# Halved attention scores spread into a dense layer, and two reorderings of v pieces, in a one-core attention and dense kernel

## Chip, cores, metric

One core of one Trainium2 chip. The metric is the device time of one execution in microseconds (us), lower is better. Times of a kernel are medians over several executions. Ratios are the mean time of one kernel's fast runs over that of the other's fast runs of the same rounds, so they are not quite the ratios of the medians quoted.

Names in the profiles: PE is the matrix engine (PEld its weight loads), ACT and DVE are the two engines that in these kernels read PSUM, the memory that PE's results go to here, and apply exp, relu, sums and copies ("eviction" is such a copy out of PSUM), POOL is a fourth engine. The number in brackets at the end of a line is the idle time of the engine before it, and what ended it.

## The reference

Block-sorted attention, then a dense layer with a squared relu. Cut to what matters:

```python
# q, k, v: 4 batches x 8 heads x 768 x 64; sort_net: 4 x 8 x 8 x 8 ; block = 96 rows
P = sinkhorn(sort_net)                       # five rounds of row and column normalising
k_sorted = einsum('bhij,bhjcd->bhicd', P, k_b); v_sorted = the same with v_b
scores = scale * q_b @ k_sorted.T            # within each block of 96
attn = exp(scores - max) / sum
x = attn @ v_sorted                          # -> 3072 tokens x 512
out = (s * relu(x @ w_in)**2 + b) @ w_out    # 512 -> 2048 -> 512
```

## The kernel before

A batch of 768 tokens is two half batches (`t`) of four blocks. `s_piece` makes scores and exp for one pair of heads (`hp`) of a half batch, `p_piece` the weighted values ("pv") and their normalisation into x, `t_piece` the transposes of x, `ffn1` the first dense matmuls ("hps"), relu and square ("gt"), `ffn2` the second ("ops"). Attention of later half batches runs in `slot()`, between the matmuls of dense layers. All PSUM tiles come from two pools: `psa`, three buffers of 2 x 512 floats a row, and `psb`, two buffers of 512 floats a row.

```python
psa = tile_pool(name="psa", bufs=3, space=PSUM);  psb = tile_pool(name="psb", bufs=2, space=PSUM)

def s_piece(t, hp):                               # 8 matmuls, one exp of 96 x 768
    sc = psa.tile([BLK, 2, 512], FP, tag="a", name="sc")
    ...                                           # matmul per block n and head e of the pair
    at = atp.tile([BLK, 2, TG], BF, tag="at", name="at")
    nc.scalar.activation(out=at, in_=sc[:, :, 0:TG], func=AF.Exp, scale=scale)

def p_piece(t, hp, n0=0, nn=HB):                  # blocks n0 .. n0+nn
    if nn < HB: p1 = psb.tile(...)                # two blocks: the small pool
    else:       p2 = psa.tile(...)                # four blocks: the large pool
    ...                                           # matmuls at x vs
    nc.vector.reciprocal(out=rec, ...)
    nc.vector.tensor_tensor(out=x[...], in0=pv, in1=rec, op=ALU.mult)

def ffn1(t, slot=nothing, n0=0, nn=HB):
    for f0 in range(0, NF, 2):                    # 8 steps
        hps = psa.tile([128, 2, 512], FP, tag="a", name="hps")
        ...                                       # 8 matmuls
        nc.scalar.activation(out=rt, in_=hps, func=AF.Relu)
        nc.vector.tensor_tensor(out=gt, in0=rt, in1=rt, op=ALU.mult)
        slot()

# start: ... k and v pieces of batch 0, s_piece(0, 0..3) among the last v pieces, then the ladder:
for hp in range(NHP):
    p_piece(0, hp, 0, 2)
    if hp == 3: t_part(0, 0, "s", 0, 2)
    warm_up(2, psa)                               # two matmuls of 128 x 256 on zeros
t_part(0, 2, "v", 0, 2); warm_up(2, psa)
ffn1(0, Queue([P(0,0,2,2), P(0,1,2,2), P(0,2,2,2), P(0,3,2,2),
               q_half(1), t_piece(0,"v",2,2), SC(1,0), SC(1,1)], 8), 0, 2)   # blocks 0, 1
ffn1(0, Queue([...], 8), 2, 2)                                               # blocks 2, 3
...
# k pieces of batch 1 in ffn2(0): evicted by "vsv"[c0 // 32], v = DVE, s = ACT
```

The softmax here doesn't subtract the row's maximum and nothing guards it: scores larger than these inputs give would overflow.

## Time and profile before

| | before |
|---|---|
| median of 5 runs | 233.47 us (233.34 to 233.67) |
| span of the profiled run | 231.6 us |
| first pv matmul / first hps matmul | 23.71 / 27.32 us |
| fifth hps group / q transposes of the second half | 30.84 / 31.60 us |
| hps of the next dense layer | 47.08 us |
| ops matmuls behind the wait on ot | 70.32 us |

The positions are starts on PE. As PE is busy for 97% of the span, the difference of two such starts against another kernel tells what was won or lost between them. The lines of the profile that carry the argument are in the prediction.

### The profile page before, as it was taken

To read this page: it belongs to the slowest core of one execution; us is meant where nothing else is said; L and a number is where in the kernel's file an instruction comes from. 1 tells how busy PE (TensorE), PEld (TensorE's weight loads), DVE (VectorE), ACT (ScalarE), POOL (GpSimd) and SP (SyncE) were. 2 spreads that over 40 slices of the span, in tenths; PEclk is the share of its full clock that TensorE was granted. 3 is DMA by queue.
4 is the path that set the end of the run, shared out by engine and by line. 5 is a ranking of instruction groups with operands and counts; after the bars stand their busy time and mean duration, and the time that the engine had idled before them with its cause. 6 is when DMAs were issued, how large, how long until landed. Compare 5 with 4: busy or idle time off the path is not lost.

```text
span 231.6 us, 4837 instructions
## 1 busy us (share of the span) xinstructions
PE 224.3 (97%) x2036; PEld 136.8 (59%) x2036; DVE 116.8 (50%) x245; ACT 114.6 (49%) x164; POOL 48.3 (21%) x62
## 2 busy tenths in 40 slices
PE   8879999999999999999999999999999999999994
PEld 6779887765544555566555555665555556554442
DVE  5778566638992645244446653343452634432221
ACT  6168479685158486856630645656222236660000
POOL 7820000399992000007920000000000000000000
PEclk9975699999999999999999999999999999999999
DMA  5999999998799992764999995610115240001212
GB/s 93 142 200 211 226 193 205 231 220 183 106 110 180 273 312 63 161 82 65 130 148 133 183 197 115 93 47 0 46 47 113 93 110 4 3 0 45 80 59 91
DMA packets 46695, 28.90 MB, mean 125 GB/s; under 512 B 35921, under 2 KB 41041, under 8 KB 46161
## 3 DMA queue, kind: packets, MB, share of 16 engines
q0 software_dynamic: 18800, 15.21, 47.8%
q1 hardware_dynamic: 27728, 13.32, 26.6%
q8 instruction: 16, 0.26, 0.5%
q10 hardware_dynamic: 144, 0.07, 0.1%
q14 instruction: 7, 0.05, 0.1%
HBM read 29.63 MB, written 8.65 MB: 165 GB/s over the span
## 4 chain that ended last, share of the span: by engine, by line
PE 82%; DVE 7%; DMA 5%; ACT 3%; issue 1%; POOL 0%; POOLq 0%
PE hps L473 35%; PE ops L516 31%; DMA qr<-in_q_dram 5%; PE pv L402 4%; PE sc L375 3%; DVE gt L478 2%; ACT ks L240 2%; DVE ks L238 2%; PE tv L320 2%; PE ops L501 2%; PE tk L294 1%; PE tv L350 1%; PE wp L182 1%; PE tq L254 1%; PE tv L336 1%
## 5 line engine op out<-in xcount | busy, mean ns | idle before, releaser
L473 PE MATMUL hps<-xt,wi 128*128 128x384 bf16 (+1 forms) x576 | 87.1, 309 | 0.3 <-ACT rt L477 0.3
L516 PE MATMUL ops<-wo,gt 128*128 128x512 bf16 x368 | 86.9, 380 | 0.4 <-DVE ot L490 0.4
L473 PEld LDWEIGHTS <-wi 128*128 128x128 bf16 x576 | 54.1, 98 | 30.6 <-issue 1.3
L477 ACT ACTIVATE rt<-hps 128x768 bf16<-128x768 f32 (+1 forms) x72 | 53.1, 741 | 37.4 <-PE hps L473 37.0
L478 DVE TENSOR_TENSOR gt<-rt 128x768 bf16<-128x768 bf16 (+1 forms) x72 | 41.2, 574 | 50.2 <-ACT rt L477 50.0
L516 PEld LDWEIGHTS <-gt 128*128 128x128 bf16 x368 | 33.6, 98 | 37.2 <-issue 1.0
L378 ACT ACTIVATE at<-sc 96x768 bf16<-96x768 f32 x32 | 24.4, 804 | 27.7 <-PE sc L375 27.7
L490 DVE SCALAR_TENSOR_TENSOR ot<-ops,s_bc,bias 128x512 f32<-128x512 f32 x23 | 17.1, 749 | 41.2 <-PE ops L516 41.2
L240 ACT CAST ks<-tk 64x512 bf16<-64x512 f32 (+1 forms) x32 | 18.6, 582 | 10.5 <-PE tk L294 10.2
L407 DVE TENSOR_TENSOR x<-pv,rec 96x512 bf16<-96x512 f32 (+1 forms) x36 | 22.6, 627 | 1.3
L639 POOL TENSOR_TENSOR csum<-csum,wo 128x512 f32<-128x512 f32 x14 | 17.6, 1254 | 1.0
L402 PEld LDWEIGHTS <-at 96*128 96x128 bf16 (+1 forms) x256 | 12.0, 104 | 3.8
L182 PE MATMUL wp<-zt 128*128 128x256 bf16 x86 | 12.9, 311 | 1.1 <-DVE warm L113 1.1
L238 DVE CAST ks<-tk 64x512 bf16<-64x512 f32 (+1 forms) x20 | 13.0, 651 | 1.1 <-PE tk L294 0.8
L402 PE MATMUL pv<-vs,at 96*128 96x66 bf16 (+1 forms) x256 | 13.0, 199 | 0.1
L240 ACT CAST vn<-tv 128x512 bf16<-128x512 f32 (+1 forms) x12 | 9.4, 799 | 7.2 <-PE tv L350 5.0
L375 PEld LDWEIGHTS <-ks 64*96 64x96 bf16 x256 | 8.6, 128 | 5.8 <-issue 5.1
L406 DVE RECIPROCAL rec<-pv 96x8 f32<-96x8 f32 (+1 forms) x36 | 6.9, 192 | 9.5 <-PE pv L402 9.4
L84 POOL DMA_DIRECT2D qr<-in_q_dram x12 | 10.6, 912 | 4.8 <-DMA kb<-in_k_dram 3.1
L375 PE MATMUL sc<-qt,ks 64*96 64x96 bf16 x256 | 10.9, 219 | 0.1
L182 PEld LDWEIGHTS <-zt 128*128 128x128 bf16 x86 | 9.0, 110 | 2.6 <-DVE warm L113 1.1
L294 PEld LDWEIGHTS <-kb 64*128 64x128 bf16 x192 | 6.7, 99 | 3.9 <-issue 3.4
(73 smaller groups left out, 98.4 us busy)
## 6 DMA issues: line engine op xcount, KB each, us to landing
out_dram<-ot SPq DMA_DIRECT2D x23, 256.0 KB, 2.4
kb<-in_k_dram POOLq DMA_DIRECT2D x4, 768.0 KB, 12.2
vb<-in_v_dram POOLq DMA_DIRECT2D x4, 768.0 KB, 19.0
wi<-in_moe_w_in_dram POOLq DMA_DIRECT2D x2, 1024.0 KB, 19.7
wo<-in_moe_w_out_dram POOLq DMA_DIRECT2D x2, 1024.0 KB, 32.6
qr<-in_q_dram POOLq DMA_DIRECT2D x12, 128.0 KB, 13.5
dv<-vn SPq DMA_DIRECT2D x6, 256.0 KB, 7.5
vs<-dv POOLq DMA_DIRECT2D x4, 384.0 KB, 12.7
```

What stands on the lines that cost most here:

```text
L182: nc.tensor.matmul(out=wp, lhsT=zt[:, 0:128], rhs=zt, start=True, stop=True)
L238: nc.vector.tensor_copy(out=out, in_=in_)
L240: nc.scalar.copy(out=out, in_=in_)
L375: nc.tensor.matmul(out=sc[:, e, n * BLK:(n + 1) * BLK], lhsT=ks[pr, g0 + n, :], rhs=QT[b][pr, hp, q0:q0 + BLK], start=True, stop=True)
L378: nc.scalar.activation(out=at, in_=sc[:, :, 0:TG], func=AF.Exp, scale=scale)
L402: nc.tensor.matmul(out=pv[e][0:m, (n - n0) * VW:(n - n0 + 1) * VW], lhsT=atf[:, c0:c0 + m], rhs=VS[b][:, gi, :], start=True, stop=True)
L407: nc.vector.tensor_tensor(out=x[:, n0:n0 + nn, hp * 128:(hp + 1) * 128].rearrange("p n (e d) -> p e n d", e=2), in0=pvv[:, :, :, 0:D], in1 ...
L473: nc.tensor.matmul(out=hps[:, f, 0:nt], lhsT=wi_at(hp, f0 + f), rhs=xt_at(t, hp, n0, nn), start=(hp == 0), stop=(hp == NHP - 1))
L477: nc.scalar.activation(out=rt[:, :, 0:nt], in_=hps[:, :, 0:nt], func=AF.Relu)
L478: nc.vector.tensor_tensor(out=gt[:, f0:f0 + 2, c0:c0 + nt], in0=rt[:, :, 0:nt], in1=rt[:, :, 0:nt], op=ALU.mult)
L516: nc.tensor.matmul(out=ops, lhsT=gt[:, f, m * 128:(m + 1) * 128], rhs=wo_at(f), start=(f == 0), stop=(f == NF - 1))
L639: nc.gpsimd.tensor_tensor(out=csum, in0=csum, in1=wo_at(f), op=ALU.add)
```

## The change

The first scores are made in halves (two blocks each), so that only the halves which the ladder needs come before it. The other halves move into the first half of the dense layer, two pairs of heads in each of the first two steps; the second pv pieces, one per step before, then come two per step. Two reorderings sit next to waits: pv of pair 2 ahead of a v piece of batch 1, and a v piece of the later batches ahead of scores. The diff, cut to its core:

```diff
+    def s_half(t, hp, n0, nn=2):
+        sc = psa.tile([BLK, 2, 512], FP, tag="a", name="sc")
+        ...                                  # 4 matmuls
+        at = atp.tile([BLK, 2, nn * BLK], BF, tag="at", name="ath")
+        nc.scalar.activation(out=at, in_=sc[:, :, 0:nn * BLK], func=AF.Exp, scale=scale)
+        AT[t, hp, n0] = at
 # p_piece reads AT[t, hp, n0] where there is one
-    s_piece(0, 0)            # and pairs 1, 2, 3, among the last v pieces
+    s_half(0, 0, 0)          # the same
-    ffn1(0, Queue([P(0, 0, 2, 2), P(0, 1, 2, 2), P(0, 2, 2, 2), P(0, 3, 2, 2),
+    def SH(hp): return lambda: (s_half(0, hp, 2), s_half(0, hp + 1, 2))
+    ffn1(0, Queue([SH(0), SH(2), seq(P(0, 0, 2, 2), P(0, 1, 2, 2)),
+                   seq(P(0, 2, 2, 2), P(0, 3, 2, 2)),
                    lambda: q_half(1, "s"), lambda: t_piece(0, "v", 2, 2), SC(1, 0), SC(1, 1)], 8), 0, 2)
-    ... seq(SC(1, 3), P(1, 1)), V1(1), P(1, 2), P(1, 3), ...
+    ... seq(SC(1, 3), P(1, 1)), P(1, 2), V1(1), P(1, 3), ...
-    ... V2[0], S2(2, 0), V2[1], S2(2, 2), V2[2], V2[3], ...
+    ... V2[0], V2[1], S2(2, 0), V2[2], S2(2, 2), V2[3], ...
```

More of the change, by code (lines that the diff above doesn't have):

```diff
@@ L379, in s_piece @@
         AT[t, hp] = at
+    def s_half(t, hp, n0, nn=2):
+        b, half = divmod(t, 2)
+        g0 = (b % 2) * 32 + hp * NB + half * HB
+        sc = psa.tile([BLK, 2, 512], FP, tag="a", name="sc")
+        for n in range(n0, n0 + nn):
+            for e in range(2):
+                pr = slice(e * 64, (e + 1) * 64)
+                q0 = (half * HB + n) * BLK
+                nc.tensor.matmul(out=sc[:, e, (n - n0) * BLK:(n - n0 + 1) * BLK],
+                                 lhsT=ks[pr, g0 + n, :], rhs=QT[b][pr, hp, q0:q0 + BLK],
+                                 start=True, stop=True)
+        at = atp.tile([BLK, 2, nn * BLK], BF, tag="at", name="ath")
+        nc.scalar.activation(out=at, in_=sc[:, :, 0:nn * BLK], func=AF.Exp, scale=scale)
+        AT[t, hp, n0] = at
     def p_piece(t, hp, n0=0, nn=HB):
         b, half = divmod(t, 2)
-        at = AT[t, hp]
+        halved = (t, hp, n0) in AT
+        at = AT[t, hp, n0] if halved else AT[t, hp]
         if t not in X:
@@ L398, in p_piece @@
             for n in range(n0, n0 + nn):
-                c0 = (e * HB + n) * BLK
-                m = 128 if c0 + 128 <= 2 * TG else BLK
+                c0 = (e * nn + n - n0) * BLK if halved else (e * HB + n) * BLK
+                m = 128 if c0 + 128 <= at.shape[1] * at.shape[2] else BLK
                 gi = e * 32 + hp * NB + half * HB + n
@@ L594 @@
     v_piece0(32, 16, "v")
-    s_piece(0, 0)
+    s_half(0, 0, 0)
     v_piece0(48, 8, "v")
-    s_piece(0, 1)
+    s_half(0, 1, 0)
     v_piece0(56, 8, "v")
-    s_piece(0, 2)
-    s_piece(0, 3)
+    s_half(0, 2, 0)
+    s_half(0, 3, 0)
     for hp in range(NHP):
@@ L619, in V1, with SH @@
         return lambda: v_piece1(i * 8, eng)
-    ffn1(0, Queue([P(0, 0, 2, 2), P(0, 1, 2, 2), P(0, 2, 2, 2), P(0, 3, 2, 2),
+    def SH(hp):
+        return lambda: (s_half(0, hp, 2), s_half(0, hp + 1, 2))
+    ffn1(0, Queue([SH(0), SH(2), seq(P(0, 0, 2, 2), P(0, 1, 2, 2)),
+                   seq(P(0, 2, 2, 2), P(0, 3, 2, 2)),
                    lambda: q_half(1, "s"), lambda: t_piece(0, "v", 2, 2), SC(1, 0), SC(1, 1)], 8), 0, 2)
-    ffn1(0, Queue([seq(SC(1, 2), P(1, 0)), V1(0), seq(SC(1, 3), P(1, 1)), V1(1), P(1, 2), P(1, 3),
+    ffn1(0, Queue([seq(SC(1, 2), P(1, 0)), V1(0), seq(SC(1, 3), P(1, 1)), P(1, 2), V1(1), P(1, 3),
                    seq(V1(2), V1(3)), lambda: t_piece(1, "v")], 8), 2, 2)
@@ L652 @@
                + [lambda c0=c0: k_piece(1, c0, 16, 1, "vsv"[c0 // 32])() for c0 in range(0, BLK, 32)]
-               + [seq(lambda: load_q(2), lambda: load_k(*brows(2)), bias_piece), V2[0], S2(2, 0), V2[1], S2(2, 2), V2[2], V2[3],
+               + [seq(lambda: load_q(2), lambda: load_k(*brows(2)), bias_piece), V2[0], V2[1], S2(2, 0), V2[2], S2(2, 2), V2[3],
                   P2(2, 0), V2[4], P2(2, 2), V2[5], S2(3, 0),
```

## The prediction

> **What bounds the kernel now.** I read the page first (who is busy), then the waits of PE, the granted clock in narrow windows, and the timeline from 12 to 100 us, the only part that the change touches.
>
> ```profile
> PE 224.3 (97%) x2036; PEld 136.8 (59%) x2036; DVE 116.8 (50%) x245; ACT 114.6 (49%) x164; POOL 48.3 (21%) x62
> ```
>
> PE is the bound over the whole span, so a change is worth what it removes from PE's queue or from PE's waits, and costs what it adds there. The waits of PE are few; these two lie where the change acts:
>
> ```profile
> PE ops L516 <- DVE ot L490: 0.4, 1, 0.4
> PE hps L473 <- ACT rt L477: 0.3, 1, 0.3
> ```
>
> The timeline puts the 0.3 us wait before the matmuls at 42.99 us and the 0.4 us wait before those at 70.32 us. So the reorderings that the description calls "around waits" can win 0.9 us at the very most (counting by starts, 42.52 to 42.99 and 69.91 to 70.32). The windows show where PE runs at half clock:
>
> ```profile
> 14.00:16.00 2.00, 1.51 (x33) 1.35 (x28) 1.93 (x3) 1.99 (x4) 0.00 (x0) 0.53 0.95 157
> ...
> 26.00:28.00 2.00, 2.00 (x19) 1.70 (x17) 1.01 (x4) 0.48 (x1) 0.00 (x0) 0.56 1.21 246
> 28.00:30.00 2.00, 2.00 (x33) 1.86 (x31) 1.04 (x4) 0.98 (x2) 0.00 (x0) 1.00 1.01 203
> ```
>
> The first of the last three numbers is the granted clock: half from 14.2 us to about 27.9 us, full afterwards. The stage before the dense layer lies in the slow stretch, and what ends it is not the scores but v:
>
> ```profile
> 21.36 0.81 ACT L378 ACTIVATE at<-sc 96x768 bf16<-96x768 f32 x1 [0.65 <-PE sc L375]
> ...
> 22.97 0.69 DVE L238 CAST vs<-tv 96x512 bf16<-96x512 f32 x1 [0.20 <-PE tv L320]
> ...
> 23.71 0.38 PE L402 MATMUL pv<-vs,at 96*128 96x66 bf16 x4
> ```
>
> The first exp is done at 22.17 us, the last v eviction at 23.66, and the weighted values start at 23.71. From there to 27.32 the stage is a fixed ladder of pv, warm-up and transposes on PE, 0.65 us a step.
>
> Then the dense layer's first half, in which the second scores will have to go:
>
> ```profile
> 27.32 1.05 PE L473 MATMUL hps<-xt,wi 128*128 128x192 bf16 x8
> 28.20 0.30 PE L402 MATMUL pv<-vs,at 96*128 96x66 bf16 x4
> 28.34 0.83 PE L473 MATMUL hps<-xt,wi 128*128 128x192 bf16 x8
> 29.00 0.30 PE L402 MATMUL pv<-vs,at 96*128 96x66 bf16 x4
> ...
> 30.84 0.83 PE L473 MATMUL hps<-xt,wi 128*128 128x192 bf16 x8
> 31.60 0.94 PE L254 MATMUL tq<-ident,qr 64*64 64x64 bf16 x48
> ```
>
> By starts, eight hps matmuls occupy PE 0.66 us (28.34 to 29.00), four pv ones 0.14. A step is 0.80 to 0.88 us, and nothing waits more than 0.1. The pieces that feed ACT and DVE there, by form between 20 and 48 us:
>
> ```profile
> L477 ACT ACTIVATE rt<-hps 128x384 bf16<-128x384 f32 x16 | 7.8, 497 | 4.9 <-PE hps L473 4.6
> L378 ACT ACTIVATE at<-sc 96x768 bf16<-96x768 f32 x8 | 6.4, 808 | 1.0 <-PE sc L375 1.0
> ...
> L407 DVE TENSOR_TENSOR x<-pv,rec 96x256 bf16<-96x256 f32 x8 | 3.4, 420 | 0.3
> ```
>
> [...] The trace agrees (497 and 808), so I take 0.49 us for a halved exp, some 0.45 in a row. [...] the trace shows it where a ready normalisation waits behind the relu's square (pv of 41.31 us, its reciprocal at 42.31 after the square of 42.04). That order is what the step below rests on.
>
> **Part 1: the first scores in halves.** Four of eight matmuls and half of each exp leave the stage before the dense layer: 16 matmuls, some 0.8 us of PE at half clock (eight take 0.40 us there), and 4 x (0.81 - 0.49) = 1.3 us of ACT. On the path lies only this: the last v matmuls come eight sc matmuls, 0.4 us, earlier, but DVE is evicting the piece before until 22.78, so its 0.20 us of idle is all that is won. The dense layer then begins at 27.13 instead of 27.32, still at half clock: the 0.19 us is worth 0.09 us of work at full clock. Its first eight matmuls end at 28.11 instead of 28.20.
>
> **Part 2: the second halves in the dense layer.** Added to PE: 16 matmuls at full clock, 0.31 us for eight: 0.62 us. Added to ACT: four exps, two behind each of the first two relus. The scores and hps share three buffers of the large PSUM pool (pv pieces of two blocks use the small one, of two). Before, hps had all three to itself; now each step wants hps, sc, sc, so every next hps must wait for the relu of the one before. Step by step, with 0.2 us from the last matmul's issue to ACT:
> - hps0 ends 28.11; sc, sc to 28.42; relu0 28.31 to 28.80; exps to 29.25 and 29.69.
> - hps1 waits for relu0: 28.84 instead of 28.42 (wait 0.42), to 29.50. relu1 29.70 to 30.19. sc, sc 29.58 to 29.90, the second waiting for the second exp. Exps to 30.64 and 31.08.
> - hps2 waits for relu1: 30.23 (0.33), to 30.89. relu2, behind two exps, 31.09 to 31.58. Its square 31.62 on DVE.
> - The two pv pieces now together: PE 30.97 to 31.25. Their normalisations stand behind the square on DVE: first x done 32.51, second 33.06 (reciprocal and product some 0.55 us apart).
> - hps3 31.25 to 31.91. The next two pv pieces need the small pool's two buffers back: 32.55 (wait 0.64) and 33.10 (0.41), to 33.24.
> - hps4 at 33.32; it was 30.84.
>
> So +2.48 us at hps4: 0.62 of moved work, 1.80 of waits (0.42 + 0.33 + 0.64 + 0.41), 0.15 of seams between pieces, less 0.09 won before. ACT is the cause of the first half of the waits (seven ACTIVATEs in a row, 28.31 to 31.58, while PE from 28.11 to 30.89 has 1.94 us of work), the small pool of the rest. From hps4 on the order is the old one, so the shift stays.
>
> **Part 3: pv of pair 2 ahead of v piece 1.** By the old clock: the pv piece moves from 41.31 to 40.31, the next hps waits for the product of 40.74 (0.2 us), but PE reaches the following pv at 42.53 with a free buffer, and the hps at 42.99 starts at 42.80. The wait of 0.47 us becomes one of 0.2 and the gain is 0.19 us.
>
> **Part 4: v piece 1 ahead of scores 2.** DVE's row of evictions ends at 68.70 and bias and ot follow until 70.28, whatever PE does. Before the wait PE now does two matmuls (0.43 us) in place of sixteen (0.49 and a wait of 0.17); the sixteen come after it. It loses 0.06 us.
>
> Sum: 2.48 - 0.19 + 0.06 = +2.35 us, 235.8 us. DMA, POOL's sums and DVE's long row from 53.8 to 70.3 us start from PE's results and move with it. I take 235.6, since a replay by hand rather over-counts waits.
>
> **Rivals.** (a) *The scores hide.* If ACT kept up and buffers came free in time, only 0.62 - 0.09 - 0.19 + 0.06 = +0.4 us would be left, 233.9 us. For it: ACT is idle 4.6 us before relus between 20 and 48 us. Against: that idle lies in single steps of 0.3 us, and the four exps come in two steps in a row. (b) *The author's gain:* v is ready sooner, the late waits go, and the moved matmuls fill holes: -0.3 to -0.9 us, 232.6 to 233.2. Against: the first half has no holes of PE to fill, and the waits to be won add up to 0.9. (c) *The clock falls:* [...] Against: at 60 to 72 us PE works through similar small pieces and the clock stays at 1.00.
>
> **Range and chances.** Replay 235.6; (a) and (b) together a fifth, (c) a twentieth. Range 233.4 to 236.7. Faster by over 2% would need 4.7 us, five times all waits to be won: 0.005. Slower by over 2% is 238.1, beyond (c): 0.025. Within: 0.97.
>
> **What would show it.** In the profile after: the last v eviction at about 23.47 us with no idle before it; new waits of hps on relu near 28.8 and 30.2 us; pv waiting for x near 32.5 and 33.1; the tq matmuls (31.60 before) at about 34.1; the wait on the relu at 42.99 gone or halved; the wait on ot at 70.3 (now near 72.6) still there, not smaller. I am wrong if the tq matmuls come before 33 us, if hps runs on without waits while the exps are pending, or if the clock rises in another window than at 27.9.

Rival (c) would cost, in sum, 237.3 us; the "beyond (c)" of the chances means that sum. The 497 and 808 ns are the means of the lines L477 and L378 above, and two relus of 384 elements in a row take 0.89 us (from 33.97), so some 0.45 each. From the last matmul's issue to ACT it is 0.20 us (the hps group of 28.34 is issued by 29.00, its relu starts at 29.20). As to order: on DVE it is the normalisation named in the prediction; on ACT it is a relu: the hps group of 32.48 is issued by 33.14 but its relu starts at 33.97, behind the q copy of 33.28 (0.80 us). That the slow stretch of the clock would end at the same time as before, on which the 0.09 us of part 1 rests, was the assumption; it ended at 27.77 us before and at 28.31 after.

## The result, and the profile after

The changed kernel takes 236.21 us (median of 5, 235.58 to 236.44) against 233.47 us, ratio 1.0112 (95% interval 1.0095 to 1.0128): 1.1% slower. The prediction said 235.6 with 97% for "within 2%".

PE is the bound as before, but is busy for a smaller share. Part 1 of the page after, and three of the waits of PE (us in total, times, longest):

```profile
PE 224.0 (95%) x2016; PEld 137.1 (58%) x2036; DVE 117.7 (50%) x245; ACT 114.8 (49%) x168; POOL 48.2 (21%) x62
```

```profile
PE pv L419 <- DVE x L424: 0.9, 2, 0.6
...
PE ops L533 <- DVE ot L507: 0.6, 1, 0.6
PE hps L490 <- ACT rt L494: 0.5, 2, 0.3
```

Over the whole span PE's busy time is the same (224.3 us before, 224.0 after), so in sum it is idle time that was added. That sum hides two things: work left a stage in which PE now waits for v instead, and it came into a stage in which PE had no idle time. So each stage is read by itself. The stage before the dense layer, after (start, duration, instruction, idle before it):

```profile
21.32 2.47 DVE L238 CAST vs<-tv 96x1024 bf16<-96x1024 f32 x3 [0.68 <-PE tv L320]
...
23.84 0.40 PE L419 MATMUL pv<-vs,ath 96*128 96x66 bf16 x4 [0.38 <-DVE vs L238]
```

The three last v evictions now run in one row with no idle between them, as predicted, and PE waits 0.38 us for them. Then the first half of the dense layer, where before had steps of 0.80 to 0.89 us after the first:

```profile
27.55 1.20 PE L490 MATMUL hps<-xt,wi 128*128 128x192 bf16 x8
...
28.68 0.38 PE L390 MATMUL sc<-qt,ks 64*96 64x96 bf16 x8
28.78 0.49 ACT L494 ACTIVATE rt<-hps 128x384 bf16<-128x384 f32 x1 [1.69 <-PE hps L490]
28.98 0.10 PEld L490 LDWEIGHTS <-wi 128*128 128x128 bf16 x1
...
29.32 0.82 PE L490 MATMUL hps<-xt,wi 128*128 128x192 bf16 x8 [0.27 <-ACT rt L494]
...
30.18 0.49 ACT L494 ACTIVATE rt<-hps 128x384 bf16<-128x384 f32 x1 [0.15 <-PE hps L490]
...
30.72 0.82 PE L490 MATMUL hps<-xt,wi 128*128 128x192 bf16 x8 [0.27 <-ACT rt L494]
...
33.06 0.31 PE L419 MATMUL pv<-vs,ath 96*128 96x66 bf16 x4 [0.58 <-DVE x L424]
...
33.70 0.30 PE L419 MATMUL pv<-vs,ath 96*128 96x66 bf16 x4 [0.32 <-DVE x L424]
...
33.83 0.83 PE L490 MATMUL hps<-xt,wi 128*128 128x192 bf16 x8
...
34.59 0.94 PE L254 MATMUL tq<-ident,qr 64*64 64x64 bf16 x48
```

All four waits that the prediction named are there: two of hps on relu and two of pv on x. Note the ACT line at 30.18: the second relu waited 0.15 us for PE, not PE for ACT.

One ruler has to be kept for waits. A group of eight hps matmuls is listed with 0.83 us, but the next group can start 0.66 us after its start, as matmuls overlap. The bracket counts from the listed end, so it is less than what is lost by starts. At 28.98 the weights for the second hps group are loaded; it starts at 29.32: 0.34 us lost by starts, 0.27 in the bracket. By starts the four waits are 0.34, 0.34, 0.75 and 0.49 us (in the brackets 0.27, 0.27, 0.58 and 0.32). The prediction's replay counts by starts.

Durations by form confirm the cost of a halved exp (the last number before the bar's end is the mean in ns, between 20 and 52 us):

```profile
L494 ACT ACTIVATE rt<-hps 128x384 bf16<-128x384 f32 x16 | 7.8, 497 | 6.0 <-PE hps L490 5.8
...
L394 ACT ACTIVATE ath<-sc 96x384 bf16<-96x384 f32 x8 | 3.6, 483 | 1.2 <-PE sc L390 1.0 <-PE tv L320 0.3
```

The starts on PE, side by side, show where the time came from:

| start of | before | after | shift | change of shift |
|---|---|---|---|---|
| hps, first group | 27.32 | 27.55 | 0.23 | |
| hps, fifth group | 30.84 | 33.83 | 2.99 | +2.76 |
| transposes of x, second half | 44.96 | 47.80 | 2.84 | -0.15 |
| hps of the next dense layer | 47.08 | 50.03 | 2.95 | +0.11 |
| ops behind the wait on ot | 70.32 | 73.31 | 2.99 | +0.04 |
| hps of the third dense layer | 92.38 | 95.54 | 3.16 | +0.17 |
| end of the span | 231.57 | 234.74 | 3.17 | +0.01 |

The first 0.23 us is not a cost of the change: in this execution the first v eviction starts at 19.42 us, before at 18.98, and that start differs by 0.2 us between executions of kernels with the same front. So this pair of profiles overstates the slowdown; the ratio over the runs, some 2.6 us, is the measure. With equal starts of that eviction the front can be compared: from 18.98 the first pv is at 23.71 in the kernel before and at 23.50 in run 6 below (same front as the change); from 19.18 it is at 23.85 in run 1 (old front) and at 23.61 in run 3 (new front). The halving brings the first pv 0.21 to 0.24 us forward.

**Two clock states.** The windows of the profile after show the granted clock (first of the last three numbers) rising later than before:

```profile
26.00:28.00 2.00, 2.00 (x20) 1.69 (x18) 1.22 (x4) 0.48 (x1) 0.00 (x0) 0.50 1.25 254
28.00:30.00 2.00, 1.73 (x23) 1.44 (x21) 0.36 (x1) 1.22 (x3) 0.00 (x0) 0.92 1.01 204
```

In the traces the slow stretch of the clock at the start, at 0.50 of full speed, is 10.24 us long (16.56 to 26.80 us in run 9) or 13.65 us (14.11 to 27.77 us before, 14.65 to 28.31 after); the difference, 3.41 us, is called a window here. In the three windows ahead of 27.77 us before, PE's records cover 3.27, 3.32 and 3.41 us. The mean clock of an execution, which is listed for each, is near 0.978 with the shorter stretch (0.975 to 0.978) and near 0.971 with the longer (0.968 to 0.971); almost all executions have one of these values (the exceptions are in runs 8 and 12). The kernel before is in both: its 20 runs near 0.978 average 233.23 us and its 13 runs near 0.971 average 233.61. As effects of 0.2% are at stake, I compare runs of equal clock where both have some:

| kernel | runs near 0.978 | runs near 0.971 |
|---|---|---|
| before | 233.23 (20) | 233.61 (13) |
| the change | 235.76 (2) | 236.33 (3) |
| reorderings only | 233.32 (3) | 233.85 (3) |
| halves only | 235.71 (2) | 236.29 (2) |
| spread, first form | 236.16 (1) | 236.20 (3) |
| pair in one tile | none | 235.85 (4) |
| spread, mended | 234.99 (4) | 235.20 (2) |
| pv spread alone | 235.25 (2) | 235.72 (3) |
| scores spread alone | 235.89 (3) | 236.34 (1) |
| no second scores | 233.80 (3) | 233.96 (3) |
| third k piece on ACT | 232.60 (4) | 233.13 (2) |
| the same and pv reordered | 232.69 (4) | 232.85 (2) |

At equal clock the change costs 2.53 or 2.72 us.

### The profile page after: what moved, and what is told of

Same layout as the page of the kernel before. It is cut to its first block, busy times and chain, and to the rows that moved or that the text cites. A ratio compares the mean times of both kernels' runs of the same rounds, so it can differ in the third digit from the quotient of the medians.

```text
span 234.7 us, 4822 instructions
## 1 busy us (share of the span) xinstructions
PE 224.0 (95%) x2016; PEld 137.1 (58%) x2036; DVE 117.7 (50%) x245; ACT 114.8 (49%) x168; POOL 48.2 (21%) x62
## 4 chain that ended last, share of the span: by engine, by line
PE 78%; DVE 13%; ACT 5%; issue 2%; DMA 1%
PE hps L490 33%; PE ops L533 31%; PE pv L419 3%; DVE gt L495 3%; PE sc L375 3%; ACT ks L240 2%; DVE ks L238 2%; ACT rt L494 2%; PE ops L518 1%; PE tk L294 1%; PE tv L320 1%; DVE vs L238 1%; DVE x L424 1%; PE wp L182 1%; DMA sn<-in_sort_net_dram 1%
## 5 line engine op out<-in xcount | busy, mean ns | idle before, releaser
L533 PE MATMUL ops<-wo,gt 128*128 128x512 bf16 x349 | 83.8, 380 | 2.0 <-DVE ot L507 0.6
L495 DVE TENSOR_TENSOR gt<-rt 128x768 bf16<-128x768 bf16 (+1 forms) x72 | 41.7, 581 | 52.4 <-ACT rt L494 52.2
L378 ACT ACTIVATE at<-sc 96x768 bf16<-96x768 f32 x28 | 21.3, 803 | 27.5 <-PE sc L375 27.5
L419 PEld LDWEIGHTS <-at 96*128 96x128 bf16 x224 | 9.6, 102 | 3.0
L419 PE MATMUL pv<-vs,at 96*128 96x66 bf16 x224 | 10.1, 195 | 0.0
L375 PEld LDWEIGHTS <-ks 64*96 64x96 bf16 x224 | 6.4, 121 | 5.7 <-issue 5.6
L375 PE MATMUL sc<-qt,ks 64*96 64x96 bf16 x224 | 8.2, 210 | 0.1
```

Of the source, the lines that this page charges most:

```text
L375: nc.tensor.matmul(out=sc[:, e, n * BLK:(n + 1) * BLK], lhsT=ks[pr, g0 + n, :], rhs=QT[b][pr, hp, q0:q0 + BLK], start=True, stop=True)
L419: nc.tensor.matmul(out=pv[e][0:m, (n - n0) * VW:(n - n0 + 1) * VW], lhsT=atf[:, c0:c0 + m], rhs=VS[b][:, gi, :], start=True, stop=True)
L495: nc.vector.tensor_tensor(out=gt[:, f0:f0 + 2, c0:c0 + nt], in0=rt[:, :, 0:nt], in1=rt[:, :, 0:nt], op=ALU.mult)
L533: nc.tensor.matmul(out=ops, lhsT=gt[:, f, m * 128:(m + 1) * 128], rhs=wo_at(f), start=(f == 0), stop=(f == NF - 1))
```

## The experiments

My theory: doing the second scores two at a time makes waits for PSUM buffers, ACT and DVE in the dense layer, and that is most of the cost. Rivals: the moved work itself, the reorderings, or the clock.

**1. Reorderings only** (the kernel before with the last two hunks of the diff).

> The two reorderings without the halved scores. My prediction's sum gives -0.19 (pv of pair 2 ahead of v piece 1) + 0.06 (v piece 1 ahead of scores 2) = -0.13 us, 233.3 us, ratio 0.9994. The profile after suggests less: there the shift against before fell by 0.15 us over the first reordering and grew by about 0.17 us over the second, so -0.0 us, ratio 1.000. Rival (the author's gain): both waits of before go, -0.5 to -0.9 us, ratio 0.996 to 0.998.

Measured: 233.49 us, before 233.36; ratio 1.0004 (0.999 to 1.0018). No gain. The wait on relu at 42.99 us is gone from its profile, but the wait it was to shorten later is longer:

```profile
70.40 1.02 PE L516 MATMUL ops<-wo,gt 128*128 128x512 bf16 x4 [0.61 <-DVE ot L490]
```

It was 0.41 us before. The gain hoped for (ratio 0.996 to 0.998) is outside the interval: the waits were there, but reordering did not remove the time.

**2. Halves only** (the change with those two hunks undone).

> Only the halved scores, both reorderings undone. My prediction gives 2.48 us over before, 236.0 us, ratio 1.0106, that is the whole slowdown of the change. Rival: the reorderings have a part in the slowdown (pv pieces and v pieces colliding with the shifted work), then this is clearly under 1.010.

Measured: 235.87 us, ratio 1.011 (1.0094 to 1.0126). Within the interval, the whole slowdown is the halving.

**3. Spread, first form.** One halved score per step, one pv piece per step:

```diff
-    ffn1(0, Queue([SH(0), SH(2), seq(P(0,0,2,2), P(0,1,2,2)), seq(P(0,2,2,2), P(0,3,2,2)),
-                   q_half(1), t_piece(0,"v",2,2), SC(1,0), SC(1,1)], 8), 0, 2)
+    ffn1(0, Queue([S1(0), S1(1), seq(S1(2), P(0,0,2,2)), seq(S1(3), P(0,1,2,2)),
+                   seq(P(0,2,2,2), q_half(1)), P(0,3,2,2), seq(t_piece(0,"v",2,2), SC(1,0)), SC(1,1)], 8), 0, 2)
```

> The change with the same instructions, but one halved score per hps step in four steps and one pv piece per step, never two. If the slowdown is waits for buffers and for ACT and DVE made by doing two at once, nearly all 1.8 us of them go and only the moved PE work stays: +0.4 to +0.6 us over before, 233.9 to 234.1, ratio 1.002 to 1.003. Rival: the moved work itself is the cost (more ACTIVATEs, matmuls that do not fill holes, narrower weights), or the clock: then it stays near 1.010.

Measured: 236.19 us, ratio 1.0118 (1.0105 to 1.0131), where I had expected 1.002 to 1.003: nothing won, which by itself spoke for the rival. But the profile shows the four waits gone and a single new one:

```profile
36.87 0.26 PE L447 MATMUL tr<-ident,x 96*128 96x96 bf16 x2 [1.10 <-DVE x L424]
```

I had put the last pv piece behind the q copies, which hold ACT for 1.50 us from 33.98; the relus queue behind them (35.37), the square behind the relu (35.91), and the last x behind the square (36.39). The transposes then wait for x. One wait had been traded for another, so this run decides nothing.

**4. Pair in one tile.** Two head pairs' second scores in one PSUM tile and one exp:

```diff
-    def SH(hp): return lambda: (s_half(0, hp, 2), s_half(0, hp + 1, 2))
+    def SH(hp): return lambda: s_pair(0, hp, 2)   # one psa tile, 8 matmuls, one exp of 96 x 768
```

> The change, but the second scores of two head pairs share one tile of the large PSUM pool and one exp of 96x768 in place of two of 96x384. The hps of each step then has a free buffer. If the large pool's three buffers make the waits of hps on relu, those two waits (0.27 us each in the profile after) go; the waits of pv for x (0.58 and 0.32 us) stay nearly as long, because they hang on relu, square and products in a row. By a replay hps4 comes 0.4 us earlier than in the change: 235.7 us, ratio 1.0095. Rival (the row of ACT alone holds it): ACT has 0.9 instead of 0.81 us per pair, so 0.1 to 0.2 us are won and the waits on relu stay.

Measured: 235.85 us, ratio 1.0103 (1.009 to 1.0117). All its runs are near 0.971, where the change has 236.33: 0.5 us won, in line with the 0.4 expected. No hps wait on relu is left in its profile; pv still waits, 0.69 and 0.17 us in the brackets:

```profile
29.02 0.83 PE L513 MATMUL hps<-xt,wi 128*128 128x192 bf16 x8
...
32.55 0.28 PE L442 MATMUL pv<-vs,atq 96*128 96x66 bf16 x4 [0.69 <-DVE rec L446]
```

ACT is hardly relieved by it (one exp of 0.80 us for two that take 0.86 in a row), and in the profile of the change the second relu waited for PE. So it was the three large buffers, and not ACT's rate, that made the waits on relu.

**5. Spread, mended.** As 3, with the last pv piece ahead of the q copies, which move a step later, and both groups of scores in the last step (the transposes stay in the seventh step, unlike what the expectation says):

```diff
-                   seq(P(0,2,2,2), q_half(1)), P(0,3,2,2), seq(t_piece(0,"v",2,2), SC(1,0)), SC(1,1)], 8), 0, 2)
+                   P(0,2,2,2), seq(P(0,3,2,2), q_half(1)), t_piece(0,"v",2,2), seq(SC(1,0), SC(1,1))], 8), 0, 2)
```

> The spread version again, mended: in its first form the waits on buffers and ACT were gone from the profile, but a new wait of 1.1 us stood in their place, the transposes for the last pv piece, which I had put behind the q copies. Here that piece stands ahead of the q copies and the transposes a step later. If the waits are the cost, 1.0 us of the first form goes and what stays is the moved work with its seams (0.62 us, plus 0.3 by the steps of 0.98 us that the first form showed where before had 0.80): +0.9 to +1.3 us, 234.3 to 234.7 us, ratio 1.004 to 1.006. Rival (the moved work and the clock are the cost, waits only fill time that is lost anyway): over 1.009.

Measured: 235.08 us, ratio 1.0078 (1.0066 to 1.009): above the 1.004 to 1.006 that I expected. At equal clock it is 0.8 to 1.1 us faster than the change and 1.6 to 1.8 us slower than before. Its PE timeline shows what the moved work costs with no wait around it, and the one wait that my order brought:

```profile
28.28 0.29 PE L390 MATMUL sc<-qt,ks 64*96 64x96 bf16 x4
28.50 0.83 PE L490 MATMUL hps<-xt,wi 128*128 128x192 bf16 x8
29.27 0.29 PE L390 MATMUL sc<-qt,ks 64*96 64x96 bf16 x4
...
37.24 0.83 PE L490 MATMUL hps<-xt,wi 128*128 128x192 bf16 x8 [0.48 <-DVE xt L238]
```

Four sc matmuls take 0.22 us (28.28 to 28.50), and after hps (0.66 us from 28.50) a seam of 0.11 us passes before the next sc. Four such groups with their seams are 1.3 us. The change has two groups of eight (0.31 us each) and two seams, 0.8 us: spreading makes the moved work itself dearer by 0.5 us. At 36.09 sixteen sc matmuls follow (twice 0.31 us), and the next hps group starts 1.15 us later: by starts 0.53 us are lost to xt. So of the 1.9 us of waits in the change, which are all gone, 0.5 come back as smaller groups and 0.5 as a new wait, and about 0.9 are won.

Against before: from its first hps group (27.45) to the q transposes (33.44) six groups take 5.99 us; before takes 4.28 us for five (27.32 to 31.60), 4.94 with a sixth of 0.66. That is 1.05 us more (less than 1.3, as before loses some 0.2 us of its own there, most of it to the clock in its first group). With the 0.53 and the 0.17 of the last reordering it makes up the 1.6 to 1.8 us.

**6. pv spread alone.**

```diff
-    [SH(0), SH(2), seq(P(0,0,2,2), P(0,1,2,2)), seq(P(0,2,2,2), P(0,3,2,2)), q_half(1), t_piece(...), SC(1,0), SC(1,1)]
+    [SH(0), SH(2), P(0,0,2,2), P(0,1,2,2), P(0,2,2,2), seq(P(0,3,2,2), q_half(1)), seq(t_piece(...), SC(1,0)), SC(1,1)]
```

> The change, but the second pv pieces come one per step instead of two per step; the scores stay two per step. By the replay of my prediction, the waits of pv for x (0.64 and 0.41 predicted, 0.58 and 0.32 seen) go, those of hps for relu stay: 0.9 to 1.1 us less than the change, 235.1 to 235.3, ratio 1.007 to 1.008. Rival: the pv pieces wait for x anyway since the squares are late: no gain, 1.011.

Measured: 235.65 us, ratio 1.0098 (1.0085 to 1.0112): 0.5 to 0.6 us won at equal clock, about half of what I expected. Its profile has no pv wait on x; the relu waits stay (0.24 and 0.27), and a new one of 0.18 us on the q copies appears, which my replay had not seen. By starts PE loses 0.24 us there and 0.20 us one group later, so of the 1.24 us taken away some 0.44 come back, and 0.1 as a seam between the transposes and the scores that follow them.

**7. Scores spread alone.**

```diff
+    [S1(0), S1(1), S1(2), seq(S1(3), P(0,0,2,2), P(0,1,2,2)), seq(P(0,2,2,2), P(0,3,2,2)), q_half(1),
+     seq(t_piece(...), SC(1,0)), SC(1,1)]
```

> The change, but the second scores come one per step; the pv pieces stay two per step, one step later. By replay the waits of hps for relu (0.27 us twice) go, those of pv for x stay: 0.5 to 0.9 us less than the change, 235.3 to 235.7, ratio 1.008 to 1.0095. With the former run: if each gain stands alone, the sum of the two is what the mended spread version wins; if they overlap, it wins less than the sum.

Measured: 236.01 us, ratio 1.0119 (1.0104 to 1.0133): nothing won, an expectation missed. Its profile has no wait on relu, and pv waits for x with 0.26 and 0.32 us in the brackets, 0.43 and 0.49 by starts, where the change loses 0.75 and 0.49. So by starts 1.0 us of waits is gone, and still nothing is won. The same trace shows where it went. Four groups of four sc take 1.3 us with their seams instead of 0.8. And behind the q copies PE waits as in run 6 (eight sc matmuls take 0.31 us, here 0.55 and 0.51 pass):

```profile
36.03 0.38 PE L375 MATMUL sc<-qt,ks 64*96 64x96 bf16 x8
36.58 0.82 PE L490 MATMUL hps<-xt,wi 128*128 128x192 bf16 x8 [0.18 <-ACT qt L240]
37.33 0.38 PE L375 MATMUL sc<-qt,ks 64*96 64x96 bf16 x8
37.84 0.83 PE L490 MATMUL hps<-xt,wi 128*128 128x192 bf16 x8
```

Those are 0.5 and 0.44 us, together what was taken away. So this run doesn't isolate the waits on relu. The two spreads together (run 5) win 0.8 to 1.1 us, more than the sum of the two alone (0.5 and nothing). By the same count that is because runs 6 and 7 pay 0.44 us each behind the q copies and run 5 pays 0.53 once. This is an account from the traces; no run tests it by changing the place of the q copies alone.

**8. In the ladder.** The second scores take the place of one of the two warm-ups in each step of the ladder; dense queue as before, only the pv reordering kept:

```diff
         if hp == 3: t_part(0, 0, "s", 0, 2)
-        warm_up(2, psa)
+        s_half(0, hp, 2)
+        warm_up(1, psa)
```

> A version that should beat the change: the second halves of the scores go into the ladder before the dense layer, each in the place of one of two warm-up matmuls of 128x256 (four sc matmuls of 96 columns, 0.2 us at half clock, for one warm-up of 0.21 us). The dense layer's queue is that of before; pv of pair 2 stays ahead of v piece 1, v piece 1 of batch 2 goes back. If moved work and its waits are the whole cost, this is at 233.2 to 233.5, ratio 0.999 to 1.0005, since the ladder's step is set by the products on DVE (0.63 us) as much as by PE. Rival: with fewer dense warm-ups the clock rises a window of 3.4 us later and PE works on at half clock: +1 to +1.7 us, ratio 1.004 to 1.007, with a clock below 0.965.

Measured: 235.99 us, ratio 1.0105 (1.0084 to 1.0125), where I had expected 0.999 to 1.0005. None of its six runs has a clock near 0.978, where before has 7 of 11 in the same rounds: three are near 0.971 (235.33 us on average, from 234.85 to 236.18) and three at 0.962 to 0.964, by that value a window longer in the slow state (236.02). The slow stretch of its profile ends at 29.83 us, later than before (27.77), after (28.31) and in runs 9 (26.80) and 12 (29.03). So the rival on the clock holds: with fewer warm-ups the slow stretch tends to be a window longer. But even without it my size was wrong. A step of the ladder, in a run near 0.971:

```profile
23.81 0.39 PE L390 MATMUL sc<-qt,ks 64*96 64x96 bf16 x4
...
24.14 0.40 PE L182 MATMUL wp<-zt 128*128 128x256 bf16 x1
...
24.33 0.46 PE L419 MATMUL pv<-vs,ath 96*128 96x66 bf16 x4
```

At half clock four sc matmuls take 0.33 us (23.81 to 24.14), where I had put 0.2, and there is a seam in front of them; the step is 0.90 us instead of 0.67, some 0.9 us in four steps.

**9. No second scores** (a change of meaning: the second pv pieces read the first exps again; it still passed the comparison with the reference, probably because the exps of such small scores are all near one another, which no run tested).

```diff
-        at = AT[t, hp, n0] if halved else AT[t, hp]
+        at = AT[t, hp, 0] if halved else AT[t, hp]
 # and the dense queue of before, no SH
```

> A wrong result on purpose: the change without its second scores at all (the second pv pieces read the first exps again, one per step as before), both reorderings kept. It measures what the halving wins in front, free of what it costs inside. My prediction gives 0.09 us for it; with the reorderings at +0.1 us by their own run, ratio 0.999 to 1.001, 233.0 to 233.5 us. Rival (the halving is a real gain in front that the dense layer eats up): 16 matmuls and 1.3 us of ACT less show as -0.5 us or more, ratio under 0.998.

Measured: 233.79 us, ratio 1.0024 (1.0002 to 1.0046). I had expected a ratio of 0.999 to 1.001. One run, 234.87 us, is 1.5 us above the two others of its clock, so a loss is not certain; a gain of 0.5 us, the rival, is excluded. With the second halves left out altogether, the kernel is still not faster than before: nothing is left of what the front won. One reason is probably in the ladder: halved exps make the last of four weights 96 columns wide. In the stretch of the ladder the profile of the change has:

```profile
L419 PEld LDWEIGHTS <-ath 96*128 96x128 bf16 x11 | 1.1, 131 | 0.8 <-issue 0.3
L419 PEld LDWEIGHTS <-ath 96*96 96x96 bf16 x4 | 0.7, 186 | 0.0
```

186 ns instead of 131, once per step, and a step takes 0.67 us (24.05 to 24.72 in the change) instead of 0.65. From the first pv to the first hps it is 3.71 us in run 3 against 3.61 in run 1: of 0.24 us, 0.14 is left, and that at half clock. Why the narrower load takes longer there, no run here isolates.

**10. Third k piece on ACT** (the kernel before, one letter changed).

```diff
-  "vsv"[c0 // 32]
+  "vss"[c0 // 32]
```

> The kernel before with one line changed: the third k piece of batch 1 is evicted by ACT, not DVE. Part 4 of my prediction says that DVE's row of evictions, then bias and ot, sets the wait of 0.41 us at 70.3 us whatever PE does. Then four evictions of 0.7 us leave that row, bias and ot are done before PE needs the buffer, and both the 0.41 us and the 0.17 us inside the scores ahead of it go: -0.4 to -0.6 us, ratio 0.9975 to 0.9983. Rival: another wait stands right behind (the ACT evictions end no earlier than 68.4 us and the scores wait for them): ratio 0.999 to 1.000.

Measured: 232.71 us, before 233.47 in the same rounds; ratio 0.9971 (0.9956 to 0.9986), a little more than the 0.9975 to 0.9983 expected. Bias and ot are early, and PE goes on without a wait:

```profile
67.49 0.75 DVE L561 TENSOR_SCALAR bias<-bps,b_bc 128x512 f32<-128x512 f32 x1 [1.28 <-PE bps L560]
...
68.28 0.75 DVE L490 SCALAR_TENSOR_TENSOR ot<-ops,s_bc,bias 128x512 f32<-128x512 f32 x1
...
70.03 1.04 PE L516 MATMUL ops<-wo,gt 128*128 128x512 bf16 x4
```

Bias now waits for PE (1.28 us), where before it stood behind four evictions. This beats both kernels.

**11. The same, with pv of pair 2 reordered.**

> The former, with the change's first reordering (pv of pair 2 ahead of v piece 1). The profile of the reorderings alone showed 0.15 us won by it and 0.11 given back at the start of the next dense layer, which waits for the eviction of the transposes on DVE: so no more than 0.05 us beyond the former run. If the prediction's 0.19 us stays, ratio 0.9965 to 0.9975.

Measured: 232.75 us, ratio 0.9969 (0.9955 to 0.9983). Not told apart from run 10: the first reordering is worth nothing that can be measured.

**12. In the ladder, no warm-ups** (run 8 without its `warm_up(1, psa)`).

> The second scores in the ladder again, with no warm-up matmuls beside them. With one warm-up each, a step took 0.90 us instead of 0.67, as four sc matmuls take 0.33 us at half clock with their seam, and the clock rose at 29.8 us. If only the length of the step cost time, the step is 0.67 again and the run is at 233.3 to 233.7, ratio 1.000 to 1.001. If the warm-ups are what brings the clock back, it rises a window or two later and the run is at 235 to 236.5, with a clock of 0.964 or less.

Measured: 234.59 us, ratio 1.0052 (1.0033 to 1.007). The step is 0.68 us again (24.13 to 24.81), the first hps group starts at 27.21, yet the clock rises only at 29.0 us (before 27.8) and the first two hps groups run slowly (1.29 and 0.80 us from start to the next piece, 0.66 at full clock). Five of six runs are near 0.971 (234.57 on average), one is at 0.962 and none near 0.978, where before has 6 of 11. So, as in run 8, the slow stretch tends to be one window longer, not two; the time lies between the two forecasts, and neither holds as I put it. Against before at 0.971 it is 1.0 us slower; about 0.6 of that can be the later rise (1.26 us more at half clock), the rest stays open.

## Why the prediction was right

**Verdict and size.** "Within 2%" was right, and 236.21 lies in the range. The replay's own sum, 235.8, was nearer than the 235.6 I gave; taking 0.2 us off because a replay by hand "rather over-counts waits" went the wrong way: the waits were under-counted, 1.80 us against 1.92.

**The front (part 1).** Right: the v evictions set the stage, they run without idle, and the first pv comes 0.21 to 0.24 us sooner, where I had 0.19. But the ladder is 0.10 us longer, which fits the narrower weights (186 ns against 131) that I did not count, and of the 0.09 us at full clock nothing is to be seen in the times of run 9.

**The dense layer (part 2).** Right in the sum and in its terms. From first to fifth hps group I had +2.67 us (6.19 against 3.52): 0.62 of moved work, 1.80 of waits, 0.15 of seams, 0.10 of clock. The profile shows +2.76. Counted by starts, as the replay counts: two groups of eight sc, 0.62; waits of 0.34, 0.34, 0.75 and 0.49, in sum 1.92 (I had 0.42, 0.33, 0.64 and 0.41); some 0.16 of clock, as 0.76 us of the first group run at half clock instead of 0.45; and the rest, some 0.06, for seams (two of 0.09, less what before lost between its own pieces). So two thirds of the added time are waits. (With the brackets of the profile in place of starts the waits would seem to be 1.44 us, and 0.48 us would wrongly be put down to seams.) What the replay did not foresee is the price of spreading: run 5 shows that the moved work costs 1.3 us in four groups and not 0.8.

**The cause named for the waits on relu fell in part.** The replay has the right reason: hps, sc and sc share three buffers, so hps waits for the relu before it. The summary then says "ACT is the cause of the first half of the waits", as relus stand behind exps. In the profile the first two relus wait for PE, not for an exp, and run 4, which leaves a large buffer free in each step, removes both waits while ACT has nearly the same work. So the buffers make them, and ACT's row does not. Also, I took the waits off one by one; runs 6 and 7 show that each new order of the queue brings costs of its own, so the gain is not the wait that goes.

**The reorderings (parts 3 and 4).** The gain of 0.19 us is 0.15 in the profile, but 0.11 is given back at the next dense layer, whose first matmuls wait for DVE's eviction of the transposes; I had not followed the gain to the end of the stage. The loss of 0.06 us is 0.17: one more group of scores now follows the wait instead of standing in front of it, and it costs 0.49 us and a seam of 0.10 where the v piece costs 0.43. That DVE's row alone sets the wait at 70.3 us was right; run 10 shows it by shortening the row. Two readings in the prediction are slightly off: by starts the wait there is 0.48 and not 0.41 us (PE is ready at 69.84), so the waits to be won were 0.95 us; and the slow stretch is 14.11 to 27.77 us, not 14.2 to 27.9.

**Rivals.** (a) failed by the waits; (b) failed altogether; (c) did not happen in the change: its clock has the same two values as before (0.978 and 0.971), and in its profile it is 1.00 from 28.31 us on. In runs 8 and 12, where warm-up matmuls were removed, the clock did rise later (29.83 and 29.03 us). What I had not seen is that before itself runs in two clock states, so that the time of the rise was no good sign: it is 27.77 us in the profile before (0.971), 28.31 after (0.971), and 26.80 in that of run 9 (0.978).

## What to carry to other kernels

Work moved out of a stage is worth something only if that work set the stage's end: here the v evictions did, and even leaving the moved half of the work out (run 9) won nothing. Before putting two like pieces into one step of a pipeline, count the buffers that the step uses and the work that stands in front of it on each engine; with three buffers, pieces that took two of them stopped the next step until the oldest one was read (0.34 us, twice). Spreading the pieces is not free either: each small group had its seam (0.11 us in run 5), and the engines next in the queue get other neighbours. Count predicted and measured waits by the same ruler. And a wait is removed at the engine that is late: reordering PE around DVE's row won nothing, moving the evictions of one piece off that row won 0.3%.
